# A planned gated-attention and feed-forward kernel: the plan's costs, its early fillers, the loads of step 1's gates and the places of attention's groups

## The chip, the cores and the metric

The kernel runs on one core of one Trainium2 chip. The metric is the device time of one execution in microseconds (us); of several runs the median is given. The engines have the names of the profile: PE is TensorE (PEld its weight loads), ACT is ScalarE, DVE is VectorE, POOL is GpSimd, SP is SyncE, which issues most transfers.

## The reference, cut to what matters

A gated recurrence over 768 time steps for 4 batches and 8 heads of size 48, and then a feed-forward block with 384 inputs, 2048 hidden values and 384 outputs on the 3072 resulting rows:

```python
f = 1.0 / (1.0 + np.exp(-f_logit))
for t in range(S):
    state = f[:, :, t, :, None] * state + np.einsum('bhd,bhe->bhde', k[:, :, t], v[:, :, t])
    y[:, :, t] = np.einsum('bhd,bhde->bhe', q[:, :, t], state)
...
h = x @ w_in
g = np.where(h >= 1, h, np.where(h <= -1, 0.0, (h + 1) ** 2 / 4))
out = g @ w_out
```

## The kernel before, in words

**The work.** Time is cut into 6 steps of 128. In each step the recurrence is computed in blocks: products of the gates' running values are made by two scans on VectorE (L476 and L483, `gate`), keys and queries are multiplied by them (L485, L487), and attention within a step is small products on TensorE: scores of keys and queries (L600, L666), their mask on VectorE (L631, L672), and mask times values (L721). What earlier steps add comes from a state: L753 multiplies queries by it, L814 makes what the step adds to it, out of turned keys. Keys are turned by TensorE in steps 0 and 1 (L685) and by VectorE's 32x32 transposes later (L699). A "pair" is two heads, four pairs make a step; pairs are numbered 4 times the step plus 0 to 3, and two of them are handled at a time. In step 0 the rows of the fourth pair stand in 16 spare rows of the other three tiles, and its scores are made from each of the three in turn, by `scores_of_last` (L619), here called the third-pair scores, since a product for each of the three pairs' tiles adds to them.

**The feed-forward block.** Each step has 512 columns and 16 units, 96 units in all. A unit's first half (`unit_1`, L242, unit 0 at L894) is nine wide products of 128x512, since weights and inputs are each split in a high and a low part and three of the four combinations are kept, times three blocks of 128 inputs. Then ScalarE and VectorE make the result: L245, L248 (ScalarE), the clamp L253 (VectorE), the cast to the high part `ghi` (L256, ScalarE) and the low part `glo` (L259, VectorE). The second half (`unit_2`, L266) is nine wide products again. The weights come as 64-bit numbers and are split early in the program, 25 blocks one after another: a load, a word from ScalarE (L370) and VectorE (L372), the high part (L375, ScalarE), the low part (L376, VectorE). Attention's outputs are rounded the same way into the inputs x: cast L704 on ScalarE, low half L705 on VectorE; in step 1 the outputs come in two halves of the columns, each with three casts.

**What sets the order.** A class `Plan` collects all operations with an engine, a cost from the table `COST` and what they need, and `order()` simulates the engines: at each moment a free engine takes the ready operation with the most urgent due time. The instructions are then emitted in the order of these start times, so each engine's queue is fixed. TensorE's operations are chained in the order of the calls: unit after unit, with attention's groups placed by two tables: `TURNS` says in which unit a pair's keys are turned, `VISITS` gives for each two pairs the units of the scores, of the mask times values with the state's sums, and of the outputs. An entry in the same unit as another stands directly behind it, with no wide products between.

**Fillers.** Where the plan has a gap ahead of a TensorE operation of over 500 ns, the emitting loop puts products of zeros there (`warm`, L320): as many as fill 0.9 of the gap at 330 or 230 ns each. They go to a bank that is free at the time, if there is one; from the scores of the third two heads to the first `unit_2` there is none, and none are put.

**Loads.** SyncE issues the loads in the plan's order. The gates `f` have two buffers that take turns and a third for the third load of step 0. In step 1 (`split_up`) gates, keys and queries are worked on in two halves of the columns; there a load of gates also needs `att[NP - 1]["to"]`, the moves of step 0's rows into the fourth tile `kq_71`. Three buffers `raw` take the weight blocks; a load waits for the word made from the block three before it, and the third one for step 0's last queries (L487).

Of the kernel before, what the change touches and what calls it, by code (L numbers as in the profile page):

```python
# [22 lines left out]
B, H, S, D = 4, 8, 768, 48  # L23
# [23 lines left out]

HOP, LANDING, PER_KB, NEAR, ADDING = 200, 2000, 3.0, 3500, 1500
COST = dict(mm=227, scores=1290, both=1150, part=500, states=1090, parts=850, turn=500, rows=317, scan=1145, dve=605, small=200, state=300, sums=480,
            act=710, copy=530, sig=540, issue=480, near=600, least=300)  # L50


TURNS = {4: 6, 5: 7, 6: 12, 7: 12, 8: 20, 9: 20, 10: 25, 11: 25, 12: 31, 13: 31, 14: 38, 15: 38, 16: 43, 17: 43, 18: 54, 19: 54, 20: 60, 21: 60, 22: 70, 23: 70}
VISITS = {4: (7, 10, 11), 6: (12, 13, 14), 8: (20, 23, 24), 10: (27, 28, 29), 12: (31, 35, 36), 14: (38, 40, 41), 16: (47, 51, 53), 18: (55, 57, 60), 20: (62, 69, 70), 22: (72, 74, 75)}
# [11 lines left out]


class Plan:
# [3 lines left out]
    def __init__(self):  # L72
        self.ops = []
        self.tensor = None

    def add(self, engine, cost, emit, *deps, kb=0, near=0):
# [9 lines left out]
        spread(list(deps))  # L86
        if engine == "PE":
            if self.tensor is not None and self.tensor not in flat:
                flat.append(self.tensor)
        o = Op(engine, COST[cost] if isinstance(cost, str) else cost, emit, flat, kb, near)  # L90
# [7 lines left out]
    def order(self):  # L98
        index = {o: n for n, o in enumerate(self.ops)}
        for o in reversed(self.ops):  # L100
            tail = o.cost + (LANDING + PER_KB * o.kb + (ADDING if o.engine == "POOL" else 0) if o.kb else o.near)
            o.late = min((u.late - (HOP if u.engine != o.engine else 0) for u in o.users), default=0) - tail
# [12 lines left out]
        while done < len(self.ops):  # L115
# [36 lines left out]
def gla_moe(ctx: ExitStack, tc: tile.TileContext, ff, kqd, f0, vv, vad, vbd, wd, fixedd, gates, values, headsd, out):  # L152
# [195 lines left out]

    def split_piece(k):

        j, c = order[k]

# [7 lines left out]
        mem, t = raw[k % 3][:, 0:n], bits[k % 4][:, 0:n]  # L360
# [9 lines left out]
        m = sca(COST["act"] * n // W, lambda: nc.scalar.activation(t, top, AF.Abs, bias=top_of, scale=2.0 ** 30),  # L370
# [3 lines left out]
        piece.append(v)  # L374
        h = sca("copy", lambda: nc.scalar.copy(hi, whole_val), v)  # L375
# [58 lines left out]
    def gate(m, halves=(None,)):  # L434
# [24 lines left out]
        for h, (b0, b1) in enumerate(steps):  # L459
            if split_up and h not in halves:  # L460
# [5 lines left out]
            l = dma(ft[:, cols], ff[i, p, :, cols], 256 // count, of_half(before, o, "qm") if before is not None else None,  # L466
                    att[NP - 1]["to"] if split_up else None)
# [734 lines left out]
```

## Time and profile before

| | |
|---|---|
| median of 3 runs | 481.05 us |
| lowest and highest | 479.98 and 485.14 us |
| the profiled execution's own time | 480.72 us |
| its span, first to last instruction | 478.9 us |
| busy: TensorE, VectorE, ScalarE, GpSimd | 469.0, 369.1, 265.2, 24.6 us |
| instructions | 11248 |

The span is what the profile's views cover, counted from its first instruction. A row of a timeline has the start, the length from the first start to the last end of the instructions merged in it, engine, line, operation and tiles, the shape and the count; in brackets the idle time before it and what ended that. Instructions of one engine overlap by the end of their pipeline, so the next one starts somewhat before the end that is shown; lengths of work that follows without a gap are read from start to start.

### The profile page before, as it was taken

The numbers are of one execution on the slowest core, as the hardware profiler recorded it, in microseconds if no ns is written. First come the engines' busy times: TensorE is split into PE (matmuls) and PEld (weight loads), VectorE is DVE, ScalarE is ACT, GpSimd is POOL, SyncE is SP. The second block draws the span as 40 slices with busy tenths as digits, with TensorE's granted clock in tenths as the row PEclk, the third lists the DMA queues.
The fourth block names the chain that finished last, engine by engine and source line by source line (L and its number), as shares of the span: only waits on it lengthen the run. The fifth ranks groups of instructions, "written<-read, shape, count | busy, mean of one in ns | idle before, by whom it ended". The sixth has DMA issues, their size and how long they took to land.

```text
span 478.9 us, 11248 instructions
## 1 busy us (share of the span) xinstructions
PE 469.0 (98%) x4659; PEld 384.2 (80%) x4659; DVE 369.1 (77%) x715; ACT 265.2 (55%) x487; POOL 24.6 (5%) x76
## 2 busy tenths in 40 slices
PE   8999999999999999999999999999999999999994
PEld 4788888789988888788878888888888888888883
DVE  7988989948999999999997599786576655655432
ACT  4399997856537364564654464464536344544451
POOL 3201001001000000100020000000000000000000
PEclk9999999999999999999999999999999999999999
DMA  8789754235204062131514230143420242422002
GB/s 289 219 299 310 226 193 144 69 117 214 63 15 141 3 171 73 35 122 45 133 34 151 94 119 26 45 121 112 154 89 3 89 122 88 155 88 88 2 0 73
DMA packets 21722, 54.29 MB, mean 113 GB/s; under 512 B 3328, under 2 KB 6656, under 8 KB 21664
## 3 DMA queue, kind: packets, MB, share of 16 engines
q1 hardware_dynamic: 20320, 51.43, 33.1%
q10 hardware_dynamic: 1344, 2.07, 2.0%
q8 instruction: 38, 0.62, 0.6%
q14 instruction: 20, 0.16, 0.1%
HBM read 44.63 MB, written 4.72 MB: 103 GB/s over the span
## 4 chain that ended last, share of the span: by engine, by line
PE 90%; DVE 4%; DMA 2%; ACT 2%; issue 1%; ACTq 0%; SPq 0%; DVEq 0%
PE po L266 41%; PE ph L242 39%; DMA f<-in_f 2%; PE pa L721 2%; PE pa L753 2%; PE ph L666 2%; DVE w L476 1%; DVE f L483 1%; PE pa L814 1%; PE ph L814 1%; PE pa L685 1%; DVE kq L487 1%; PE ph L894 0%; PE pa L666 0%; PE pa L863 0%
## 5 line engine op out<-in xcount | busy, mean ns | idle before, releaser
L242 PE MATMUL ph<-x,w_hi 128*128 128x512 f32 (+1 forms) x606 | 146.2, 377 | 0.0
L245 ACT ACTIVATE act<-ph,half 128x512 f32<-128x512 f32 x96 | 65.9, 687 | 111.9 <-PE ph L242 105.8
L242 PEld LDWEIGHTS ph<-x,w_hi 128*128 128x128 f32 x606 | 109.7, 188 | 20.9
L253 DVE SCALAR_TENSOR_TENSOR act<-ph,act 128x512 f32<-128x512 f32 x96 | 66.0, 687 | 52.8 <-ACT act L248 52.2
L256 ACT CAST ghi<-act 128x512 fp32r<-128x512 f32 x96 | 59.5, 620 | 67.6 <-DVE act L253 67.4
L266 PE MATMUL po<-ghi,w_hi 128*128 128x512 f32 (+1 forms) x305 | 87.1, 391 | 0.1
L266 PE MATMUL po<-ghi,w_lo 128*128 128x512 f32 (+1 forms) x305 | 83.2, 378 | 0.0
L266 PE MATMUL po<-glo,w_hi 128*128 128x512 f32 (+1 forms) x305 | 82.8, 377 | 0.0
L242 PE MATMUL ph<-x,w_lo 128*128 128x512 f32 (+1 forms) x303 | 81.2, 376 | 0.0
L259 DVE TENSOR_TENSOR glo<-act,ghi 128x512 fp32r<-128x512 f32 x96 | 65.9, 686 | 19.6 <-ACT ghi L256 18.6
L699 DVE STREAM_TRANSPOSE kn<-kq 32x128 f32<-32x128 f32 x224 | 67.8, 303 | 3.5
L266 PEld LDWEIGHTS po<-ghi,w_lo 128*128 128x128 f32 x305 | 55.2, 188 | 11.0
L266 PEld LDWEIGHTS po<-glo,w_hi 128*128 128x128 f32 x305 | 55.3, 188 | 10.9
L242 PEld LDWEIGHTS ph<-x,w_lo 128*128 128x128 f32 x303 | 55.3, 188 | 10.4
L248 ACT ACTIVATE act<-act 128x512 f32<-128x512 f32 x96 | 60.7, 632 | 2.9
L266 PEld LDWEIGHTS po<-ghi,w_hi 128*128 128x128 f32 x305 | 52.5, 188 | 10.9 <-ACT ghi L256 0.8
L386 DVE TENSOR_REDUCE ok<-raw 128x1 f32<-128x512 f32 x48 | 31.2, 678 | 4.5 <-DMA raw<-in_w 4.5
L476 DVE TENSOR_TENSOR_SCAN w<-f,least_w 128x512 f32<-128x512 f32 (+1 forms) x21 | 21.3, 1016 | 2.7 <-ACT f L474 2.2
L483 DVE TENSOR_TENSOR_SCAN f<-f,rec 128x512 f32<-128x512 f32 (+1 forms) x21 | 21.3, 1018 | 0.5
L370 ACT ACTIVATE bits<-raw,top_of 128x512 uint32<-128x512 fp8e4 (+1 forms) x25 | 18.1, 740 | 6.0 <-DMA raw<-in_w 3.4
L574 ACT ACTIVATE sd<-sd,kq 112x48 f32<-112x48 f32 x80 | 20.1, 328 | 0.0
L480 POOL COPY end<-w 128x4 f32<-128x4 f32 (+1 forms) x22 | 6.5, 295 | 261.9 <-DVE w L476 246.8
(125 smaller groups left out, 386.5 us busy)
## 6 DMA issues: line engine op xcount, KB each, us to landing
raw<-in_w SPq DMA_DIRECT2D x24, 512.0 KB, 3.5
raw<-in_w SPq DMA_DIRECT2D x21, 511.6 KB, 4.6
kq<-in_kq SPq DMA_DIRECT2D x18, 512.0 KB, 4.8
out_y<-raw SPq DMA_DIRECT2D x17, 256.0 KB, 2.2
v<-in_v SPq DMA_DIRECT2D x10, 384.0 KB, 5.0
f<-in_f SPq DMA_DIRECT2D x13, 256.5 KB, 3.0
raw<-in_w SPq DMA_DIRECT2D x4, 382.9 KB, 6.7
f<-in_f SPq DMA_DIRECT2D x7, 128.5 KB, 3.0
```

What stands on the lines that cost most here:

```text
L242: nc.tensor.matmul(ps[:, to], w_in(w_hi if high else w_lo, j, kt), xt[:, kt, t, c], start=(n == 0), stop=(n == 8))
L245: nc.scalar.activation(a, ps, AF.Relu, bias=half, scale=0.5)
L248: nc.scalar.activation(a, a, AF.Square)
L253: nc.vector.scalar_tensor_tensor(out=a, in0=ps, scalar=1.0, in1=a, op0=ALU.max, op1=ALU.min)
L256: nc.scalar.copy(hi, a)
L259: nc.vector.tensor_tensor(out=lo, in0=a, in1=hi.bitcast(F32), op=ALU.subtract)
L266: nc.tensor.matmul(po[e][:, c], w_out(part, j, e), g[:, of], start=(j == 0 and n == 0 and c.start == 0), stop=(j == NJ - 1 and n == 2))
L386: seen.append(vec("dve", lambda z=z, op=op: nc.vector.tensor_reduce(out=ok[:, 1 + NG + z + c:2 + NG + z + c], in_=words_of(raw[2])[1].bitc ...
L476: s1 = vec(1200 // count, lambda bwd=bwd, u0=u0, u1=u1: nc.vector.tensor_tensor_scan(out=wide(w[:, u0:u1]), data0=bwd, data1=wide(least_w[ ...
L483: s2 = vec(1200 // count, lambda fwd=fwd, b0=b0, b1=b1: nc.vector.tensor_tensor_scan(out=fwd, data0=fwd, data1=wide(rec[:, b0:b1]), initia ...
L574: nc.scalar.activation(ds[:, at + j * D:at + (j + 1) * D], state[:, q * B + b], AF.Copy, scale=pf[:R, j:j + 1])
L699: nc.vector.transpose(kn[n % 2][u:u + 32, ::-1, r:r + 32], src[:, :, u:u + 32])
```

## The change

It has five parts.

1. Costs. The table gets a finer set of costs; results now reach their users after a delay per engine (`LATENCY`), also on the same engine except TensorE; and passing from wide to small products on TensorE and back costs `first` and `last`.
2. Fillers. Before 20 us of the plan a gap from 250 ns on is filled whole, with one product more; behind it the rule is as before.
3. Loads. The gates of step 1 no longer need the moves of step 0; the third weight block no longer waits for step 0's last queries; the buffers of the weight blocks are followed by name (`last_in`) with the same waits otherwise.
4. The third-pair scores read 64 rows of each tile instead of 32; the rows added hold zeros on the key side.
5. `TURNS` and `VISITS` have new entries.

```diff
+LATENCY = dict(PE=235, ACT=140, DVE=110, POOL=150)
-VISITS = {4: (7, 10, 11), 6: (12, 13, 14), 8: (20, 23, 24), 10: (27, 28, 29), ...
+VISITS = {4: (6, 7, 10), 6: (11, 12, 13), 8: (18, 22, 24), 10: (24, 28, 29), ...
...
+    def lag(self, user):
+        if self.kb or self.near:
+            return HOP if user.engine != self.engine else 0
+        return 0 if self.engine == user.engine == "PE" else LATENCY.get(self.engine, HOP)
...
+            small = kind in SMALL_PRODUCTS
+            cost += (COST["last"] if small else COST["first"]) if small != self.small else 0
+            self.small = small
...
-                ready[u] = max(ready[u], end + (HOP if u.engine != o.engine else 0))
+                ready[u] = max(ready[u], end + o.lag(u))
...
-        loaded = dma(into, src, 8 * 128 * n / 1024, piece[k - 3] if k >= 3 else gates_of[2]["qm"] if k == 2 else None)
+        loaded = dma(into, src, 8 * 128 * n / 1024, last_in.get(home))
...
-            l = dma(ft[:, cols], ff[i, p, :, cols], 256 // count, of_half(before, o, "qm") if before is not None else None,
-                    att[NP - 1]["to"] if split_up else None)
+            l = dma(ft[:, cols], ff[i, p, :, cols], 256 // count, of_half(before, o, "qm") if before is not None else None)
...
-                for (_, ps, _), a in zip(last_held, (32, 96)):
-                    nc.tensor.matmul(ps[:, m], last_keys[t][a:a + 32, B - 1 - m], query(0, t, m)[a:a + 32], start=t == 0 and m == 0, stop=t == NT - 1 and m == B - 1)
+                for (_, ps, _), a in zip(last_held, (0, 64)):
+                    nc.tensor.matmul(ps[:, m], last_keys[t][a:a + 64, B - 1 - m], query(0, t, m)[a:a + 64], start=t == 0 and m == 0, stop=t == NT - 1 and m == B - 1)
...
-                if idle and o.start - idle > 500:
-                    warm(int((o.start - idle) * 0.9 / (330 if o.start < 10000 else 230)))
+                gap = o.start - idle if idle else 0
+                if o.start < 20000 and gap > 250:
+                    warm(int(gap / (330 if o.start < 10000 else 230)) + 1)
+                elif gap > 500:
+                    warm(int(gap * 0.9 / 230))
```

What it moves on the engines is shown at three places. The line numbers of the new kernel are 14 to 17 higher for the same statement there. The first is ScalarE around the rounding of step 1's first outputs (casts of pa_108 and pa_109 into x_86 and y_87; f are gates, ghi and act a unit's results, bits and w_hi weights). Before:

```order
L245 ACTIVATE act_84<-ph_112,half 128x512
L375 CAST w_hi<-bits_98 128x512
L375 CAST w_hi<-bits_95 128x512
L375 CAST w_hi<-bits_96 128x512
L704 CAST x_86<-pa_108 112x2x256
L248 ACTIVATE act_84<-act_84 128x512
L704 CAST x_86<-pa_109 112x256
L474 ACTIVATE f_67<-f_67 128x513
L474 ACTIVATE f_66<-f_66 128x513
L704 CAST y_87<-pa_109 112x256
```

Now:

```order
L262 ACTIVATE act_84<-act_84 128x512
L491 ACTIVATE f_66<-f_66 128x513
L387 ACTIVATE bits_96<-raw_92,top_of 128x512
L270 CAST ghi_89<-act_84 128x512
L387 ACTIVATE bits_97<-raw_93,top_of 128x512
L259 ACTIVATE act_83<-ph_111,half 128x512
L393 CAST w_hi<-bits_96 128x512
L262 ACTIVATE act_83<-act_83 128x512
L721 CAST x_86<-pa_108 112x2x256
L721 CAST x_86<-pa_109 112x256
L721 CAST y_87<-pa_109 112x256
```

The sigmoids of f_67 and f_66 stood between the second and the third cast; now the one of f_66 stands ahead of the casts, that of f_67 further up, and the three casts follow each other.

The second place is VectorE between the last mask of step 0 (am_77 from po_114) and the low half of unit 0's third input (x_85 from pa_108); bits and w_lo are weights, w and f_66 gates of step 1. Before:

```order
L631 TENSOR_TENSOR am_77<-po_114,fixed 128x512
L376 TENSOR_TENSOR w_lo<-bits_95,w_hi 128x3x128
L372 SCALAR_TENSOR_TENSOR bits_97<-raw_94,bits_97 128x512
L376 TENSOR_TENSOR w_lo<-bits_96,w_hi 128x3x128
L376 TENSOR_TENSOR w_lo<-bits_97,w_hi 128x512
L705 TENSOR_TENSOR x_85<-po_113,x_85 128x512
L705 TENSOR_TENSOR x_85<-pa_110,x_85 128x512
L705 TENSOR_TENSOR x_85<-pa_108,x_85 128x512
```

Now:

```order
L648 TENSOR_TENSOR am_77<-po_114,fixed 128x512
L394 TENSOR_TENSOR w_lo<-bits_95,w_hi 128x3x128
L394 TENSOR_TENSOR w_lo<-bits_96,w_hi 128x3x128
L389 SCALAR_TENSOR_TENSOR bits_97<-raw_94,bits_97 128x512
L493 SCALAR_TENSOR_TENSOR w<-f_66,least_w 128x256 x2
L394 TENSOR_TENSOR w_lo<-bits_97,w_hi 128x512
L722 TENSOR_TENSOR x_85<-po_113,x_85 128x512
L722 TENSOR_TENSOR x_85<-pa_110,x_85 128x512
L389 SCALAR_TENSOR_TENSOR bits_98<-raw_92,bits_98 128x384
L389 SCALAR_TENSOR_TENSOR bits_95<-raw_93,bits_95 128x512
L722 TENSOR_TENSOR x_85<-pa_108,x_85 128x512
```

Ahead of the third low half now stand the two scans of step 1's first gates and two more words of weight blocks.

The third place is TensorE at the end of the outputs of pairs 8 and 9 (am times v into pa) in unit 24. Before, with the second half of a unit behind them:

```order
L721 MATMUL pa_109<-am_77,v 48x64
L721 MATMUL pa_108<-am_76,v 48x64
L721 MATMUL pa_109<-am_77,v 48x64
L266 MATMUL po_113<-ghi_89,w_hi 128x512
L266 MATMUL po_114<-ghi_89,w_hi 128x512
L266 MATMUL po_115<-ghi_89,w_hi 128x512
```

Now, with the scores of pairs 10 and 11 (keys kq_70) behind them:

```order
L738 MATMUL pa_109<-am_77,v 48x64
L738 MATMUL pa_108<-am_76,v 48x64
L738 MATMUL pa_109<-am_77,v 48x64
L683 MATMUL ph_112<-kq_70 64x64
L683 MATMUL pa_110<-kq_70 64x64
L683 MATMUL ph_112<-kq_70 64x64
```

The scores of pairs 10 and 11 stood in unit 27 by themselves. The same happens with outputs and scores in units 37, 44, 54, 61 and 72. TensorE's list of products of zeros changes too: 25 ahead of the first scores, 4 ahead of the second, and 2 within the transposes of step 1's second half before; 26 ahead of the first scores, 7 ahead of the second and 5 ahead of the third now, and none behind.

## Rows read from the trace of the kernel before

**Rows 1.** the page's first part: busy time, share of the span, instructions of each engine

```profile
PE 469.0 (98%) x4659; PEld 384.2 (80%) x4659; DVE 369.1 (77%) x715; ACT 265.2 (55%) x487; POOL 24.6 (5%) x76
```

**Rows 2.** span and mean granted TensorE clock of the core

```profile
core 0: 478.9 us, clock 0.999
```

**Rows 3.** what TensorE waited for: us in total, times, longest

```profile
PE ph L320 <- DVE zeros L292: 1.0, 1, 1.0
PE pa L685 <- DVE y L705: 1.0, 1, 1.0
```

**Rows 4.** TensorE's timeline, the start: start us, us, instruction, [idle before <- releaser]

```profile
11.91 1.04 PE L320 MATMUL ph<-zeros 128*128 128x512 bf16 x4
13.19 0.37 PE L600 MATMUL po<-kq 48*128 48x128 f32 x1 [0.25 <-DVE kq L487]
...
15.73 0.37 PE L600 MATMUL po<-kq 48*128 48x128 f32 x1 [0.28 <-DVE kq L487]
...
17.91 1.09 PE L852 MATMUL po<-am,sd 128*64 128x128 f32 x16
...
26.85 0.55 PE L685 MATMUL pa<-fixed,kq 112*128 112x112 f32 x4
```

**Rows 5.** VectorE's timeline, the start

```profile
5.35 1.25 DVE L483 TENSOR_TENSOR_SCAN f<-f,rec 128x256 f32<-128x256 f32 x2
...
17.98 0.68 DVE L631 TENSOR_TENSOR act<-po,fixed 128x512 f32<-128x512 f32 x1
...
20.71 0.69 DVE L631 TENSOR_TENSOR am<-po,fixed 128x512 f32<-128x512 f32 x1
21.31 0.55 DVE L376 TENSOR_TENSOR w_lo<-bits,w_hi 128x384 fp32r<-128x384 f32 x1
21.77 0.69 DVE L372 SCALAR_TENSOR_TENSOR bits<-raw,bits 128x512 uint32<-128x512 uint32 x1
22.38 0.56 DVE L376 TENSOR_TENSOR w_lo<-bits,w_hi 128x384 fp32r<-128x384 f32 x1
...
25.49 0.69 DVE L705 TENSOR_TENSOR x<-pa,x 128x512 fp32r<-128x512 f32 x1 [0.42 <-ACT x L704]
```

**Rows 6.** ScalarE's timeline, the start

```profile
19.76 0.51 ACT L375 CAST w_hi<-bits 128x384 fp32r<-128x384 f32 x1 [2.61 <-DVE bits L372]
```

**Rows 7.** the timeline of all engines, around 85 us

```profile
82.73 0.64 ACT L474 ACTIVATE f<-f 128x513 f32<-128x513 f32 x1 [0.78 <-DMA f<-in_f]
...
83.13 0.55 PE L685 MATMUL pa<-fixed,kq 112*128 112x112 f32 x4
...
83.51 0.60 PE L320 MATMUL po<-zeros 128*128 128x512 bf16 x2
...
84.60 0.41 DVE L705 TENSOR_TENSOR y<-pa,y 112x256 fp32r<-112x256 f32 x1
...
85.07 0.79 PE L685 MATMUL pa<-fixed,kq 112*128 112x112 f32 x4 [0.96 <-DVE y L705]
```

**Rows 8.** TensorE's timeline, eight transposes without a wait

```profile
34.90 0.93 PE L685 MATMUL pa<-fixed,kq 112*128 112x112 f32 x8
```

**Rows 9.** the chain of waits around 255 us: start us, us, what

```profile
254.74 2.27 PE po L266 x9
...
259.05 2.04 PE po L266 x9
```

**Rows 10.** TensorE's timeline, nine wide products that precede small ones

```profile
75.28 1.52 PE L242 MATMUL ph<-x,w_hi 128*128 128x512 f32 x6
...
77.42 0.67 PE L753 MATMUL pa<-kq,y 48*48 48x64 f32 x32
```

**Rows 11.** the tile kq, 0 to 25 us: duration ns min/median/max, start, forms

```profile
L600 PE MATMUL pa<-kq x24: 272/272/373, 9.2 to 14.1; 48*128 48x128 f32 x24
...
L619 PE MATMUL ph<-kq,kn x24: 270/270/372, 10.8 to 17.7; 32*128 32x128 f32 x24
```

**Rows 12.** the page's DMA issues: KB each, median us from issue to landing

```profile
raw<-in_w SPq DMA_DIRECT2D x24, 512.0 KB, 3.5
```

More of the change, by code (lines that the diff above doesn't have):

```diff
@@ L45 @@
 NW = DM * DF // (128 * W)
+SMALL_PRODUCTS = ("scores", "heads", "thirds", "both", "begin", "before", "part", "states", "parts", "turn")
 HOP, LANDING, PER_KB, NEAR, ADDING = 200, 2000, 3.0, 3500, 1500
[L49 to L54, printed above, removed]
+LATENCY = dict(PE=235, ACT=140, DVE=110, POOL=150)
+COST = dict(mm=227, narrow=120, scores=1100, heads=950, thirds=1110, both=1090, begin=480, before=930, part=560, states=850, parts=830, turn=350, first=110, last=95,
+            rows=316, turned_rows=150, scan=1140, dve=602, small=200, sums=467, gate=600, act=575, bits=660, round=485, copy=520, turned=412, sig=538, decay=226,
+            issue=480, near=600, least=300)
+TURNS = {4: 5, 5: 6, 6: 11, 7: 11, 8: 15, 9: 15, 10: 24, 11: 24, 12: 30, 13: 30, 14: 37, 15: 37, 16: 44, 17: 44, 18: 54, 19: 54, 20: 61, 21: 61, 22: 72, 23: 72}
+VISITS = {4: (6, 7, 10), 6: (11, 12, 13), 8: (18, 22, 24), 10: (24, 28, 29), 12: (31, 35, 37), 14: (37, 42, 44), 16: (44, 48, 54), 18: (54, 56, 61), 20: (61, 69, 72), 22: (72, 75, 76)}
 START = (("scores", 0), ("mask", 0), ("last", 0), ("scores", 1), ("mask", 1), ("last", 1), ("scores", 2), ("last", 2), ("mask", 2),
@@ L73, in __init__ @@
         self.ops = []
-        self.tensor = None
+        self.tensor, self.small = None, False
     def add(self, engine, cost, emit, *deps, kb=0, near=0):
@@ L86, in add @@
         spread(list(deps))
+        cost, kind = COST[cost] if isinstance(cost, str) else cost, cost
         if engine == "PE":
@@ L89, in add @@
                 flat.append(self.tensor)
-        o = Op(engine, COST[cost] if isinstance(cost, str) else cost, emit, flat, kb, near)
+            small = kind in SMALL_PRODUCTS
+            cost += (COST["last"] if small else COST["first"]) if small != self.small else 0
+            self.small = small
+        o = Op(engine, cost, emit, flat, kb, near)
         for d in flat:
@@ L101, in order @@
             tail = o.cost + (LANDING + PER_KB * o.kb + (ADDING if o.engine == "POOL" else 0) if o.kb else o.near)
-            o.late = min((u.late - (HOP if u.engine != o.engine else 0) for u in o.users), default=0) - tail
+            o.late = min((u.late - o.lag(u) for u in o.users), default=0) - tail
         left = {o: len(o.deps) for o in self.ops}
@@ L347, in gla_moe @@
     SKIP = 3
+    last_in = {}
     def split_piece(k):
         j, c = order[k]
+        home = k % 3
         if c is None:
@@ L699, in emit @@
                     nc.vector.transpose(kn[n % 2][u:u + 32, ::-1, r:r + 32], src[:, :, u:u + 32])
-            c["kn"].append(vec(4 * COST["rows"], emit, c["kq"], old(n - 2, "st")))
+            c["kn"].append(vec(4 * COST["rows"] + COST["turned_rows"], emit, c["kq"], old(n - 2, "st")))
         c["tr"] = c["kn"][-1]
     def rounded(b, yf, hi, lo, y, past, cost=None):
-        eh = sca(cost or "act", lambda: nc.scalar.copy(hi, yf), y, past)
+        eh = sca(cost or "round", lambda: nc.scalar.copy(hi, yf), y, past)
         el = vec(cost or "dve", lambda: nc.vector.tensor_tensor(out=lo, in0=yf, in1=hi.bitcast(F32), op=ALU.subtract), eh)
@@ L736, in begin @@
         c["to_y"] = held, where
-        c["yb"] = add("PE", "part", attended(n, True), c["am"], c["lv"], d["lv"], [b[2] for b in held])
+        c["yb"] = add("PE", "begin", attended(n, True), c["am"], c["lv"], d["lv"], [b[2] for b in held])
     def outputs(n):
@@ L754, in emit @@
                                          start=False, stop=False)
-        c["ys"] = add("PE", 1000, emit, c["db"], d["db"], c["later"], c["yb"])
+        c["ys"] = add("PE", "before", emit, c["db"], d["db"], c["later"], c["yb"])
         y = c["y"] = d["y"] = add("PE", "part", attended(n, False), c["ys"])
```

33 lines of the change are left out of this document (17 added, 16 removed).

## The prediction

> **What bounds the kernel now.** I read the page's first part first: TensorE is busy for 469.0 of 478.9 us [rows 1], at a mean granted clock of 0.999 of full speed [rows 2], which is the 2.4 GHz level. So nothing is to be had from faster work elsewhere; only TensorE's own idle time, its own switching costs, and where its stream begins and ends can move the time. Next the list of what TensorE waited for: the two longest waits are 1.0 us each, one at the very first instruction and one at L685 [rows 3]; the others are of 0.5 us or less. Last the timelines of the stretches in which they lie: the start, up to about 27 us, where TensorE waits a quarter of a microsecond at a time for the first keys and queries [rows 4 to 6], and one place at 83 to 86 us [rows 7]. From 27 us on TensorE's products stand end to end but for that place. The reader is to see that the whole change can act on three things: that one stall, the price of passing between wide and small products, and the start.
>
> **The stall at 85 us goes: -1.8 us.** At 83.13 TensorE starts the eight transposes of step 1's second half, runs two zeros after the fourth, and then stands until 85.07; the last of the eight ends at 85.07 + 0.79 = 85.86 [rows 7]. That is 2.73 us, where eight such transposes without a wait take 0.93 us [rows 8]: 1.8 us are lost here. Why: the second four write a bank that the rounding of step 1's first outputs must leave. ScalarE's order puts two sigmoids of step 2's gates between the second and third cast of that rounding (first pair of order fences), and the second of them stood 0.78 us for its load, at 82.73; the third cast, and with it VectorE's subtraction at 84.60 that frees the bank, came later by the sigmoids and that wait [rows 7]. In the new order the three casts stand together and the sigmoid is well ahead of the first. Also, since step 1's gates no longer wait for step 0's moved rows and the second half's keys come two to three units sooner on VectorE, the load that ScalarE waited for is issued sooner relative to its sigmoid. What is late next there is the same bank: from the end of the outputs, three casts and three subtractions of 0.4 to 0.7 us each, partly side by side, an estimate of 3 us from the lengths in [rows 5, 7], against two wide runs of 2.27 and 2.04 us on TensorE [rows 9]. That leaves a microsecond or more. Bounds: -1.0 (nearly half of it comes back through another wait on the same bank) to -1.9 (the scores behind start a little before the last transpose ends).
>
> **Six small groups merge: -1.8 us.** TensorE's work is the same number of products, but the new table puts the outputs of one pair of head pairs and the scores of the next into the same unit six times (24, 37, 44, 54, 61, 72; third pair of fences); before, none coincided. A nine-product run that follows small products takes 2.27 us in the chain of waits instead of 2.04 [rows 9], and one that precedes them takes 2.14 (75.28 to 77.42) [rows 10]. So a small group standing alone costs 0.23 + 0.10 = 0.33 us in switching, and six merges save 6 x 0.33 = 2.0, less a little for the passage from outputs to scores, which the trace of before doesn't show. Small kinds that follow each other there go on at the pace of their own products, so I take -0.30 each, -1.8. If that passage cost nearly a whole edge, only 0.10 each would be left, -0.6; the upper end is -2.0.
>
> **The start: +1.1 us.** Here the change does two things against each other. VectorE's order of the first gates is tighter, so the first keys and queries are ready sooner. But TensorE is now given more zeros: 7 where there were 4 ahead of the second scores, and 5 ahead of the third scores where there were none (26 instead of 25 at the very beginning, where TensorE has to wait in any case). A zero costs 0.22 us: four last 1.04 us and two last 0.60, so two more are 0.44 [rows 4, 7]. Step by step. The four zeros from 11.91 ended at 12.95 and TensorE waited 0.25 us more, to 13.19 [rows 4]. Three more end at 12.95 + 0.66 = 13.6: the zeros overrun. Scores and third-pair scores together take 17.91 - 15.73 = 2.18 us [rows 4], so the next five zeros run from 15.8 to 16.9, and the third scores start at 16.9 instead of 15.73. Their input came at 15.73 before, and one mask of 0.60 us now stands ahead of it on VectorE: 16.3 at the latest, so the zeros alone decide. VectorE can mask these scores from about 18.05, half of 2.18 us after they start; before, it began them at 17.98, since it was itself late [rows 5]. So VectorE's lead is used up. From that mask to the last one there are the same six instructions in another order, 20.71 - 17.98 = 2.73 us [rows 5]: the last mask starts at 20.8.
>
> From there VectorE decides. Before, it began the low half of unit 0's third input at 25.49, having waited 0.42 us for the cast [rows 5]. Now four more instructions stand ahead of it (second pair of fences): two half scans of step 1's gates (1.25 us for a pair [rows 5]), a small word (0.46, as 21.31 to 21.77) and a large one (0.61, as 21.77 to 22.38) [rows 5]. With the mask (0.60), the two small low parts (0.92), a large word and a large low part (1.22) and two low halves of inputs (1.22, each taken as long as a large word), 20.8 + 0.60 + 0.92 + 1.22 + 1.22 + 1.25 + 0.46 + 0.61 = 27.1, and with its 0.69 us it ends at 27.75. The last of unit 0's nine products needs it and takes 0.23, so the transposes behind start at 27.95 instead of 26.85 [rows 4]: +1.1 us, and as TensorE's stream is dense from there on, that stays. Bounds: +0.3 (the input is ready some 0.8 us sooner, as it would be if the zeros did not overrun) to +2.0 (a load that ScalarE waits for is a microsecond later).
>
> What hides the rest. ScalarE gets step 1's four sigmoids ahead of its first weight casts; it stood idle there for 2.61 us, up to 19.76, waiting for VectorE [rows 6], and four half sigmoids are half as much. If that cover were gone (loads landing after about 20.8), every microsecond more would be on the path. The third weight block is loaded sooner and competes with nothing that is due. New costs in the plan's table change orders only.
>
> **Wider row tiles cost nothing.** The third-pair scores read 64 rows instead of 32. The medians of one product are 272 ns for 48 rows and 270 ns for 32 [rows 11], so I cost the change at zero. The Trainium skill, TensorEngine Tiling (Array Packing), section Theoretical Speedup, gives a contraction of at most 32 a packing factor of 4 and one of at most 64 only 2, which speaks against the edit. By that rule the products of these three groups could cost up to twice as much; by the rows, nothing. No row here has the same product at both widths.
>
> **The sum.** The profiled execution took 480.72 us, 1.8 us more than its span, and stands 0.33 us below the median of the three runs, 481.05. 480.7 - 1.8 - 1.8 + 1.1 = 478.2 us.
>
> **Rivals.**
> 1. The start costs little: VectorE reaches the last mask near 20.0, the low half is there 0.8 us sooner, and the start costs 0.3. 480.7 - 3.6 + 0.3 = 477.4. For it: VectorE is otherwise full in this stretch and its new order has fewer back-to-back dependences. Against: the zeros stand in TensorE's queue whatever VectorE does.
> 2. The stall comes back elsewhere: a sigmoid that waits for its load still stands in ScalarE's queue, now ahead of a unit's cast (in the first pair of fences it is ahead of the cast of a result, ghi_89). If it is 1.5 us late, the saving is gone: 478.2 + 1.5 = 479.7. Against: the load is issued about two units, some 9 us, ahead.
> 3. Slower than before: ScalarE's first cast of a unit's result now stands behind the word of a weight block whose load can only be issued once VectorE has made the word before it, at about 26.5. That load has to land by 30.5 or TensorE's first output products wait. A load of 3.5 us, the median of such blocks [rows 12], is in time. From 2.5 us late on, the kernel is slower than before; at twice the median, 7 us, it would land at 33.5, 3 us late, and the time is 478.2 + 3.0 = 481.2. For it: the DMA engines are busiest in this stretch of the program. Against: the transfers of step 1's gates, which stood ahead of such a block before, are already over.
> 4. Two products of 64 rows do run at half the pace. Each of the three groups takes 2.18 / 2 = 1.09 us [rows 4], so 3 x 1.09 = 3.3 us more on TensorE, all of it at the start: 481.5. The Trainium skill's packing factors (TensorEngine Tiling, Theoretical Speedup) would make it so. Against: the equal rows above [rows 11].
> 5. The merges save little, -0.6 in place of -1.8: 479.4.
>
> **How the numbers follow.** The forecast holds from 477.7 to 479.0, with a chance of 0.45; rival 1 0.20; rival 2 0.10; rival 3 0.05; rival 4 0.02; rival 5 0.13; something faster than all of these, under 476.2, gets 0.05. The end of the bounds on the good side is 480.7 - 1.9 - 2.0 + 0.3 = 477.1, on the bad side 480.7 - 1.0 - 0.6 + 2.0 = 481.1. A measurement differs from the profiled execution by some 0.3 us, and a start that gains rather than loses can't be excluded, so the range is 476.4 to 481.2. About 1% is what a measurement of this kernel can tell from no change: under 476.2 I give 0.08, within 1% 0.87, and above 485.9 0.05, where two of the slow rivals would have to come together.
>
> **What would show it.** Right: no zeros on TensorE behind 20 us; L685 of step 1's second half without a wait; the wide runs next to the six merged groups at 2.04 us on the side that no longer has small products; the transposes behind unit 0 at about 28.0 us; a wait of a microsecond on VectorE's third low half inside unit 0. Wrong: unit 0 ends by 27.0 (rival 1); a wait at the cast of a unit's result, or at the first output products at 31 to 34 us (rivals 2 and 3); a passage from outputs to scores of more than 0.1 us (rival 5); products of the third-pair scores that start further apart than those of the scores beside them (rival 4).

## The result, and the profile after

Each kernel was timed 20 times, in turn. The changed one took 483.90 us in the median (480.09 to 486.97), the kernel before 480.98 (479.71 to 486.70); the ratio is 1.0048 with a 95% interval of 1.0025 to 1.0072 (ratios here are estimates over the executions and not the quotients of the medians). The forecast was 478.2 us with a range of 476.4 to 481.2: the change was to gain 2.5 us against the profiled execution and lost 2.9 from median to median. The spread is part of the result. The profiled execution, 480.09 us, is the quickest of the 20, so the rows here show the change nearly at its best; a usual execution follows in the first experiment.

The page's first part, and span and clock of the core:

```profile
PE 467.6 (98%) x4666; PEld 384.4 (80%) x4666; DVE 366.5 (77%) x715; ACT 263.2 (55%) x487; POOL 28.0 (6%) x76
```

```profile
core 0: 478.3 us, clock 0.995
```

What TensorE waited for (us in total, times, longest):

```profile
PE po L280 <- ACT ghi L270: 2.3, 2, 1.6
...
PE ph L911 <- DVE x L722: 0.6, 1, 0.6
```

The wait at the transposes [rows 3] is gone. A new one leads: output products (L280) that wait for ScalarE's cast ghi of a unit's result (L270).

TensorE's timeline at the start, and VectorE's third low half of unit 0's input:

```profile
11.21 1.68 PE L334 MATMUL ph<-zeros 128*128 128x512 bf16 x7
...
14.81 1.25 PE L334 MATMUL ph<-zeros 128*128 128x512 bf16 x5
...
27.28 0.50 PE L911 MATMUL ph<-x,w_hi 128*128 128x512 f32 x1 [0.60 <-DVE x L722]
27.61 0.55 PE L702 MATMUL pa<-fixed,kq 112*128 112x112 f32 x4
```

```profile
26.54 0.68 DVE L722 TENSOR_TENSOR x<-pa,x 128x512 fp32r<-128x512 f32 x1
```

Seven and five zeros, as read from the order; the last of unit 0's products waits 0.60 us for the low half, and the transposes stand at 27.61, where 26.85 was and 27.95 was forecast. The start costs 0.76 us, from one execution of each kernel; in the second execution of the changed one (below) the transposes stand at 27.48.

TensorE's timeline at the second half of step 1: eight transposes, then scores and the next products:

```profile
79.88 0.93 PE L702 MATMUL pa<-fixed,kq 112*128 112x112 f32 x8
...
81.83 0.97 PE L280 MATMUL po<-ghi,w_hi 128*128 128x512 f32 x3
```

The same products of the kernel before start, with the zeros and the wait among them, at 83.13 [rows 7] and end ahead of this row:

```profile
86.88 0.97 PE L266 MATMUL po<-ghi,w_hi 128*128 128x512 f32 x3
```

No zeros, no wait: 81.83 - 79.88 = 1.95 us for what took 86.88 - 83.13 = 3.75. The stall is gone as forecast, 1.80 us.

The tile kq, 0 to 25 us (duration ns min/median/max):

```profile
L617 PE MATMUL pa<-kq x24: 272/272/373, 9.2 to 13.7; 48*128 48x128 f32 x24
...
L636 PE MATMUL ph<-kq,kn x24: 270/272/272, 10.2 to 17.8; 64*128 64x128 f32 x24
```

Products of 64 rows take what those of 48 take, and what those of 32 took [rows 11].

The merges, in TensorE's timeline of the kernel before around one group of outputs and one of scores (first lines of each run of nine wide products):

```profile
311.93 1.52 PE L242 MATMUL ph<-x,w_hi 128*128 128x512 f32 x6
...
317.73 1.52 PE L242 MATMUL ph<-x,w_hi 128*128 128x512 f32 x6
...
321.81 1.52 PE L242 MATMUL ph<-x,w_hi 128*128 128x512 f32 x6
...
327.21 1.52 PE L242 MATMUL ph<-x,w_hi 128*128 128x512 f32 x6
```

and of the changed kernel, where both groups stand together:

```profile
314.00 1.52 PE L256 MATMUL ph<-x,w_hi 128*128 128x512 f32 x6
...
320.73 1.52 PE L256 MATMUL ph<-x,w_hi 128*128 128x512 f32 x6
```

Before, 317.73 - 311.93 = 5.80 and 327.21 - 321.81 = 5.40 us, each with nine products of 2.04 us in front and nine behind [rows 9]: 1.72 and 1.32 us for the two groups, 3.04 together. Now 320.73 - 314.00 - 4.08 = 2.65. This merge saves 0.39 us (0.30 was forecast). Read the same way, the six merged places come to 2.65 to 2.75 us in this trace against the 3.04 of two separate groups: 0.29 to 0.39 each, 2.1 in all for the 1.8 forecast.

So the three terms came as worked out or some 0.3 us better. What was not foreseen stands eight microseconds behind that merge, in the chain of waits (start us, us, what):

```profile
317.73 5.98 DMA kq<-kq
...
323.74 2.13 DMA x<-y
...
325.88 0.70 ACT act L259
...
327.98 0.63 ACT ghi L270
...
328.65 2.34 PE po L280 x9
...
333.03 2.04 PE po L280 x9
```

Read it from the bottom. Nine output products start at 328.65 though TensorE was free 1.6 us before; they wait for ghi, ghi through VectorE's L267 for ScalarE's functions of the unit, and the first of these (L259) stood behind small copies in ScalarE's queue (x<-y, 16 rows of attention's outputs moved into the feed-forward block's inputs, issued at 323.74; they are called copies of MLP inputs below), which in turn stood until another copy, of key rows (kq<-kq) and issued at 317.73, had landed 5.98 us later.

### The profile page after: what moved, and what is told of

Read it like the earlier page. It is cut to its first block, busy times and chain, and to the rows that moved or that the text cites. A ratio compares the mean times of both kernels' runs of the same rounds, so it can differ in the third digit from the quotient of the medians.

```text
span 478.3 us, 11260 instructions
## 1 busy us (share of the span) xinstructions
PE 467.6 (98%) x4666; PEld 384.4 (80%) x4666; DVE 366.5 (77%) x715; ACT 263.2 (55%) x487; POOL 28.0 (6%) x76
## 4 chain that ended last, share of the span: by engine, by line
PE 89%; DMA 4%; DVE 2%; ACT 2%; ACTq 1%; POOL 0%; SPq 0%; issue 0%; DVEq 0%
PE po L280 41%; PE ph L256 39%; DMA f<-in_f 2%; PE pa L770 2%; PE pa L738 2%; PE ph L683 1%; DMA kq<-kq 1%; PE pa L831 1%; ACTq L298 1%; PE ph L831 1%; DVE x L722 1%; PE pa L702 1%; DVE w L493 1%; POOL kq L516 0%; PE pa L683 0%; ACT f L491 0%
## 5 line engine op out<-in xcount | busy, mean ns | idle before, releaser
L259 ACT ACTIVATE act<-ph,half 128x512 f32<-128x512 f32 x96 | 65.9, 686 | 121.2 <-PE ph L256 107.4
L267 DVE SCALAR_TENSOR_TENSOR act<-ph,act 128x512 f32<-128x512 f32 x96 | 65.9, 686 | 66.6 <-ACT act L262 65.9
L270 ACT CAST ghi<-act 128x512 fp32r<-128x512 f32 x96 | 59.6, 621 | 60.7 <-DVE act L267 60.4
L280 PE MATMUL po<-ghi,w_hi 128*128 128x512 f32 (+1 forms) x305 | 86.4, 389 | 2.3 <-ACT ghi L270 2.3
L280 PE MATMUL po<-ghi,w_lo 128*128 128x512 f32 (+1 forms) x305 | 83.1, 378 | 0.0
L280 PE MATMUL po<-glo,w_hi 128*128 128x512 f32 (+1 forms) x305 | 82.8, 377 | 0.0
L280 PEld LDWEIGHTS po<-ghi,w_lo 128*128 128x128 f32 x305 | 55.2, 188 | 10.9
L280 PEld LDWEIGHTS po<-glo,w_hi 128*128 128x128 f32 x305 | 55.3, 188 | 10.8
L280 PEld LDWEIGHTS po<-ghi,w_hi 128*128 128x128 f32 x305 | 53.0, 188 | 13.3 <-ACT ghi L270 3.1
L404 DVE TENSOR_REDUCE ok<-raw 128x1 f32<-128x512 f32 x48 | 31.1, 675 | 2.4 <-DMA raw<-in_w 2.4
L497 POOL COPY end<-w 128x4 f32<-128x4 f32 (+1 forms) x22 | 9.2, 419 | 265.1 <-DVE w L493 255.5
```

The lines of the kernel that those rows point to most:

```text
L259: nc.scalar.activation(a, ps, AF.Relu, bias=half, scale=0.5)
L267: nc.vector.scalar_tensor_tensor(out=a, in0=ps, scalar=1.0, in1=a, op0=ALU.max, op1=ALU.min)
L270: nc.scalar.copy(hi, a)
L280: nc.tensor.matmul(po[e][:, c], w_out(part, j, e), g[:, of], start=(j == 0 and n == 0 and c.start == 0), stop=(j == NJ - 1 and n == 2))
L404: seen.append(vec("dve", lambda z=z, op=op: nc.vector.tensor_reduce(out=ok[:, 1 + NG + z + c:2 + NG + z + c], in_=words_of(raw[2])[1].bitc ...
```

## The experiments

### A usual execution

The changed kernel once more.

> The changed kernel once more, so that another execution of it is profiled: its best execution was 480.1 us, as forecast, but the middle of its 20 was 483.9. Theory 'a late wait that comes and goes': a profile of a usual execution shows 2 to 5 us more idle time of TensorE than the 480.1 us one, in one or two places, and a stretch at the half clock behind it; median 483 to 485 against 480 to 482 of the kernel before. Theory 'the chip's chance': the same chain of waits, only a longer tail or a later full clock, and a median within 0.25% of the kernel before.

483.05 us (481.31 to 485.64), ratio 1.0032, 0.9998 to 1.0066. The profiled execution took 483.35 us. ScalarE's timeline in it (ACTq are issues of transfers):

```profile
320.46 0.51 ACTq L298 DMA_DIRECT2D x<-y  x1
...
321.58 2.68 ACTq L298 DMA_DIRECT2D x<-y  x2
326.88 0.51 ACTq L298 DMA_DIRECT2D kq<-kq  x1
327.44 0.69 ACT L259 ACTIVATE act<-ph,half 128x512 f32<-128x512 f32 x1 [6.12 <-DMA x<-y]
```

TensorE's wait for ghi, its timeline, and the granted clock by windows (third column from the end: 1.00 is the 2.4 GHz level, 0.50 the 1.2 GHz one):

```profile
PE po L280 <- ACT ghi L270: 3.5, 2, 3.0
```

```profile
326.35 0.84 PE L256 MATMUL ph<-x,w_lo 128*128 128x512 f32 x3
330.21 1.09 PE L280 MATMUL po<-ghi,w_hi 128*128 128x512 f32 x3 [3.02 <-ACT ghi L270]
...
333.67 1.84 PE L256 MATMUL ph<-x,w_hi 128*128 128x512 f32 x6
```

```profile
320.00:330.00 10.00, 7.20 (x32) 5.63 (x30) 4.89 (x8) 3.09 (x8) 0.00 (x0) 1.00 0.78 215
331.00:334.00 3.00, 3.00 (x8) 2.32 (x8) 2.31 (x4) 1.03 (x2) 0.00 (x0) 0.50 0.22 42
335.00:340.00 5.00, 5.00 (x24) 4.12 (x23) 3.07 (x5) 2.53 (x4) 0.00 (x0) 1.00 0.28 107
```

And the chain of waits:

```profile
320.30 6.50 DMA v<-in_v
...
330.21 3.65 PE po L280 x9
...
336.20 2.04 PE po L280 x9
```

The four issues on ScalarE run from 320.46 to 327.4, and the unit's first function comes at 327.44; the last of them, of key rows, stood until a load of values that SyncE had issued at 320.30 landed 6.50 us later. The product that the function works on was complete at about 323: TensorE's next work waits 3.02 us. Then the clock falls to half for 3.4 us of products: in the chain the same eighteen products take 336.20 - 330.21 = 5.99 us that took 333.03 - 328.65 = 4.38 in the quicker execution, 1.61 us more. 483.35 - 3.02 - 1.61 - 0.52 (the second wait for ghi, at 102 us) = 478.2: take out these three and the forecast's 478.2 is left. The quicker execution without its two waits, 1.64 and 0.66 us, leaves 477.8. 'Late wait' holds. Of the 20 executions 14 had a mean clock of 0.993 or less; this one, with a fall, had 0.992, and the quickest, without, 0.995. The kernel before has such executions too, 13 of the 35 timed beside this run; its one trace shows no fall, so what falls add to its median is not known.

Why the issues take so long is written in the program: each transfer takes the next of eight completion counters (DMAHW0 to DMAHW7) and its issue waits for the one that had that counter before. ScalarE's order with its waits, at this place:

```
363 L298 DMA x_85<-y_87 16x1024 [waits DMAHW6_49,DVE_49]
364 L298 DMA x_85<-y_87 16x1024 [waits DMAHW1_49]
365 L298 DMA x_85<-y_87 16x1024 [waits DMAHW3_49]
366 L298 DMA kq_71<-kq_68 16x1028 [waits DMAHW5_49,DMAHW4_49]
367 L259 ACTIVATE act_83<-ph_111,half 128x512 [waits PE_49]
```

The Trainium skill says in DMA: Bandwidth & Descriptors, section Anatomy of one DMA — SWDGE (gpsimd) path, that DMA engines do not wait on semaphores and that any such wait happens on the sequencer that issues. The trace agrees for ScalarE, whose transfers are not GpSimd's: 0.51 us each is what an issue takes, 5.6 and 7.0 us passed from the first of four to the function behind them.

### Which part of the change

The changed kernel has no zeros behind 20 us. Most edits below that change the planned order also leave out the rule that would put some there; of the kernels made from the changed one, only two further down, at 9 us, have any.

The table of turns and visits back to the old one (`-TURNS = {4: 5, ...}` `+TURNS = {4: 6, ...}`, and VISITS).

> The changed kernel with the old table of turns and visits, the rest as changed. If the new places of attention's groups make the time, the median falls to 480 to 481.5 us, and the six merged groups (1.8 us) are missing in the trace; if they do not, it stays at 483 to 485 or rises by the merges' 1 to 2 us.

483.61 us, 1.0033 (1.0002 to 1.0063). Not the table: the stall only moves. TensorE waits 1.28 us for ghi at 238.9, again behind a copy of key rows in ScalarE's queue, and the six merges are lost. The stall at 81 us did not come back here either.

The old rule for zeros:

```diff
-    if o.start < 20000 and gap > 250:
-        warm(int(gap / (330 if o.start < 10000 else 230)) + 1)
-    elif gap > 500: ...
+    if idle and o.start - idle > 500:
+        warm(int((o.start - idle) * 0.9 / (330 if o.start < 10000 else 230)))
```

> The changed kernel with the old rule for zeros (fewer fillers at the start: none behind the first 'last' product, fewer ahead of it). If the start's zeros make the usual execution slow, the median falls to 480 to 481 us; if they do not, it stays within 1 us of the changed kernel, and the first unit of the MLP begins 0 to 0.8 us sooner.

482.43 us, 1.0029 (0.9996 to 1.0061): not the zeros; the profiled execution waits 2.43 us for ghi at 330.66. Unit 0 did not begin sooner but 0.85 us later (25.18 against 24.33). That is not the zeros' doing: in this execution a load of the first gates landed later, and VectorE was 0.70 us behind at 10.06 already, ahead of all that it reads from TensorE. What the zeros cost at the start stays open.

The new table, in the kernel before (which so also loses its two late zeros):

> The kernel before with the new table of turns and visits alone, costs and the rest as before. If the new places are what makes a usual execution slow, this one is 2 to 4 us slower than the kernel before; by the forecast it is 0 to 2 us faster (merges), and by 'the costs set the order, not the table' it is within 1 us.

481.04 us, 0.9999 (0.9972 to 1.0025), with no wait for ghi. The merges are in it and the stall at L685 is gone, so the table alone takes that away. But the profiled execution lost 2.4 us at the start, where the clock was at half from 15.7 to 22.5 us, and from the transposes behind unit 0 on it is 1.45 us shorter than the kernel before, not 3.6: small waits in its new order, 0.51 us at 117 and 0.37 at 151 the largest, are part of what takes the rest.

The old costs and delays in the plan:

```diff
-LATENCY = dict(PE=235, ACT=140, DVE=110, POOL=150)
-COST = dict(mm=227, narrow=120, scores=1100, ... act=575, ...
+LATENCY = dict(PE=200, ACT=200, DVE=200, POOL=200)
+COST = dict(mm=227, narrow=120, scores=1290, ... act=710, ... first=0, last=0, ...
...
```

> The changed kernel with the old costs and delays in the plan (table of turns, zeros, loads and 64-row products as changed). In its order two copies of key rows and one of MLP inputs come ahead of the unit's function where the changed kernel has three and one, and two after it. If the new costs bring the wait at 328 us, it is under 0.6 us here, and the median is 480 to 481.5 us though the stall near 81 us may be back (1 to 2 us); if the wait is from the table or the loads, it stays at 1.5 to 3 us.

479.93 us (478.98 to 480.51), 0.9951 (0.9924 to 0.9979): the new costs bring the stall. ScalarE's timeline with the old ones:

```profile
322.11 2.12 ACTq L298 DMA_DIRECT2D x<-y  x2
324.57 0.69 ACT L259 ACTIVATE act<-ph,half 128x512 f32<-128x512 f32 x1 [2.16 <-PE ph L256]
...
326.84 1.16 ACTq L298 DMA_DIRECT2D kq<-kq  x2
```

The unit's function at 324.57 waits for TensorE alone: the copies of MLP inputs ahead of it are issued by 324.23, and the key rows' issues come after it. What is left of the wait for ghi stands at 328.7:

```profile
PE po L280 <- ACT ghi L270: 0.4, 1, 0.4
```

No execution had a mean clock under 0.996. Up to 320 us this kernel is 1.3 us behind the changed one (600 output products into the program, 321.09 against 319.81), so the new costs also gain something before they lose it. The stall at 81 us did not come back.

The old waits of loads (`+ att[NP - 1]["to"] if split_up else None` on step 1's gates, `piece[k - 3]` for weight blocks):

> The changed kernel with the old waits of loads: step 1's gates load only after the copies of step 0's key rows, weight blocks by the block three before. ScalarE's order around 328 us is that of the changed kernel, so by 'copies' the wait for ghi stays (1.5 to 3 us) and the median stays at 483 to 484; if sooner loads make the wait, it goes and the median falls by 2 to 3 us. Start and the place at 81 us may lose 0.5 to 2 us.

482.38 us, 0.9995 (0.9962 to 1.0029). The stall stays, 2.15 us at 328.6, and with it the fall of the clock, 328.9 to 332.3 us. Up to there this kernel is ahead of the changed one (its 451st output product starts at 243.39 against 244.88): in these two executions the sooner loads cost a little.

### The two links

Copies of key rows issued by SyncE, in the same planned order (`q = nc.sync if near == NEAR + 1 else q`), and then all small copies:

> The changed kernel, in the same planned order, but SyncE issues the copies of key rows that ScalarE issued. Theory 'copies': at 328 us ScalarE's first function of a unit stands behind three copies of MLP inputs and one of key rows, the last of which is issued only as a load of values some transfers back lands; so with the key rows' copies gone from ScalarE, TensorE's wait for the cast ghi there (1.6 us in one execution, 3.0 in another) falls below 0.5 us, no clock dip follows it, and the median falls from 483.5 to 480 to 481.5 us. Theory 'late products' (ScalarE and VectorE are simply behind there): the wait stays between 1 and 3 us and the median at 483 to 484.

> The changed kernel with all small copies, of key rows and of MLP inputs, issued by SyncE. 'Copies': the waits for the cast ghi at 102 us (0.5 to 0.7) and at 328 us both go, fastest execution 477.5 to 478.5 us, median 479 to 481; the price could be loads that queue behind twelve issues of 0.5 to 0.6 us on SyncE. 'Late products': both waits stay.

481.25 us, 0.9985 (0.9954 to 1.0017), and 480.80 us, 0.9977 (0.9946 to 1.0008): better than the changed kernel by 2 to 3 us, but a wait for ghi remains one unit later, 1.29 and 1.97 us, where 'copies' expected less than 0.5 or none. VectorE's timeline with all copies on SyncE, and TensorE behind it:

```profile
329.68 1.28 DVE L404 TENSOR_REDUCE ok<-raw 128x1 f32<-128x512 f32 x2 [4.06 <-DMA raw<-in_w]
330.87 0.68 DVE L267 SCALAR_TENSOR_TENSOR act<-ph,act 128x512 f32<-128x512 f32 x1
```

```profile
332.25 0.80 PE L280 MATMUL po<-ghi,w_hi 128*128 128x512 f32 x1 [1.97 <-ACT ghi L270]
```

A second link: two reductions (L404) that only check a weight block stand 4.06 us for its load, with the unit's L267 queued behind them. In the changed kernel the load has landed by the time these two come, behind ScalarE's delay.

Both out: copies of key rows on SyncE, and the plan counts 9 us to a checked block's landing.

```diff
-    loaded = dma(raw[2], wd[c], 8 * 128 * W / 1024, seen[-2:] or [...])
+    loaded = add("SP", "issue", lambda: nc.sync.dma_start(raw[2], wd[c]), seen[-2:] or [...], near=9000)
```

> The changed kernel with both suspected links taken out: SyncE issues the copies of key rows, and the plan counts 9 us to the landing of a weight block that is only checked, so that VectorE's two reductions of it stand later. If these two are the whole cause, TensorE waits under 0.4 us in all between 315 and 345 us, the clock does not fall there, and the median is 478 to 480 us. If only ScalarE's copies count, it is like the run with the copies moved alone, 481.3. If the stall is of another kind it comes back nearby with 1 to 3 us.

486.06 us, 1.0084 (1.0047 to 1.0122), all of it lost at the end. No wait stands between 315 and 345 us, but the checks now reach to the end of the program, and the rule for zeros filled the planned gap ahead of the product that sums them up:

```profile
462.63 7.73 PE L335 MATMUL po<-zeros 128*128 128x512 bf16 x35
470.29 0.19 PE L1003 MATMUL pa<-ones_col,ok 128*1 128x1 f32 x2
```

So 6.5 us instead, and no zeros behind 20 us:

> As the run with both links out, but the plan counts 6.5 us to a checked block's landing, so that the last check stands ahead of the 94th of 112 units. If the two links are the whole cause, no wait above 0.4 us and no fall of the clock between 315 and 345 us, last product near 469 us and a median of 477.5 to 479; if the tail was not the checks' doing, 484 to 486 again.

483.52 us, 1.0038 (1.0006 to 1.0069): a miss. In the new order copies of MLP inputs, left on ScalarE, stand ahead of the unit's function and of its square, and TensorE waits 3.69 us, with 3.4 us at half the clock behind it:

```profile
323.14 2.65 ACTq L299 DMA_DIRECT2D x<-y  x2
325.84 0.69 ACT L259 ACTIVATE act<-ph,half 128x512 f32<-128x512 f32 x1 [3.46 <-DMA kq<-kq]
329.34 0.52 ACTq L299 DMA_DIRECT2D x<-y  x1
329.90 0.63 ACT L262 ACTIVATE act<-act 128x512 f32<-128x512 f32 x1 [3.37 <-DMA kq<-kq]
```

The checks alone at 6.5 us:

> The changed kernel with the checked blocks counted at 6.5 us alone; ScalarE keeps its copies, four of them ahead of the unit's function near 328 us. By 'copies first' the wait for ghi stays at 1 to 3 us and the median at 482 to 484; if VectorE's checks were the main link, the wait goes and the median is 479 to 480.5.

482.08 us, 1.0001 (0.9967 to 1.0035), with a wait of 1.50 us for ghi at 330.9 and one of 2.03 at 251.4, where a copy of key rows stands between the function and its square in ScalarE's queue: the copies are the first link. Then both for good, all copies on SyncE and checks at 6.5 us:

> The changed kernel, new loads kept, with all small copies issued by SyncE and checked blocks counted at 6.5 us. If the two links are the whole cause, no wait above 0.8 us between 315 and 345 us and a median of 477 to 478.5 (that with old loads was 477.3; the new loads lost 0.65 us at the start). If the new loads had a part in the stall, 1 to 3 us of wait come back near 330 us and the median is 480 to 483.

478.23 us (477.05 to 479.28), 0.9907 (0.9871 to 0.9942). TensorE's waits:

```profile
PE ph L256 <- DMA x<-y: 0.8, 1, 0.8
PE pa L1002 <- DVE ok L998: 0.7, 1, 0.7
...
PE po L280 <- ACT ghi L270: 0.4, 1, 0.4
```

The wait for ghi near 330 us is gone (0.4 us are left at 31.6), the clock never falls in the trace, and the median is the forecast's 478.2. To the tenth this is luck: the order is another than the one forecast. What remains near 330 us is 0.8 us for a copy itself, which SyncE now issues later, and 0.7 at the end, for the checks.

### Teaching the plan

The plan lets no transfer issue before the eighth last has landed by its own estimate; then, an issue on ScalarE counted as 1.4 us instead of 0.6:

```diff
+    if (o.kb or o.near) and ring[-8] > t:
+        heappush(q, (ring[-8], n, o))
+        continue
```

> The changed kernel whose plan lets no transfer issue before the one eight issues back has landed by its own estimate. In its order the copy of key rows stands behind the unit's function on ScalarE, three copies of MLP inputs still ahead. If the issue that waits for the load of values is the price, ScalarE's function is 1 to 2 us sooner there, and the median falls to 480.5 to 482; if the copies of MLP inputs hold it as well, or VectorE's check is next, it stays at 482 to 484.

> The changed kernel whose plan counts 1.4 us instead of 0.6 for an issue on ScalarE (the trace: four issues took 5.6 us there). In its order two copies of MLP inputs stand ahead of the unit's function near 240 us and three near 328 us, no copy of key rows behind them. If the undercounted issue is the root, the wait for ghi falls below 0.8 us and the median to 479.5 to 481.5; if VectorE's checks are then late, 1 to 2 us of it come back and it is 481 to 483.

483.43 us, 1.0028 (0.9980 to 1.0076), and 489.42 us, 1.0150 (1.0111 to 1.0189): neither helps. In the first the copy of key rows moved from ahead of the function to between it and the square, where ScalarE stood 3.09 us; in the second, which has a copy there too, VectorE's check stood 4.41 us as well. TensorE waits 2.52 and 4.19 us for ghi there; the second loses more in smaller waits and a fall of the clock, which are not taken apart here. Both only moved the issues: a copy between a unit's product and its cast held TensorE in both.

### Combinations

Old costs with old loads; old loads with new costs, all copies on SyncE and the checks at 9 us, then at 6.5 us without late zeros:

> The kernel before with new table, zeros and 64-row products alone: old costs and old loads. The run with old costs and new loads gave 479.9. If the loads by themselves cost time at the start (0.67 us there in the run with old loads), this is 0.3 to 0.8 us below it, 479 to 479.7; if the sooner loads help step 1's first half, it is 0.5 to 1.5 us above it.

> The changed kernel with the old waits of loads, all small copies issued by SyncE, and the checks' weight blocks counted at 9 us. The run with the old loads was 1.5 us ahead of the changed kernel from 107 to 245 us and lost it in the stall near 328 us, so with both links out the last product starts near 469.5 us and the median is 477.5 to 479.5 us; if the stall only moves, 480 to 482.

> Old waits of loads, all small copies on SyncE, checked blocks counted at 6.5 us, the rest as changed. With the tail mended this keeps what the run with 9 us showed before its tail (830th output product 3.3 us ahead of the changed kernel's best execution): last product 467.5 to 468.5 us, median 475.5 to 477.5; it would be the fastest of all. If something of the tail stays, 479 to 482.

480.40 us, 0.9968 (0.9930 to 1.0007), between its two expectations and within the noise of the run with new loads; 484.58 us, 1.0054 (1.0017 to 1.0092), with the same zeros at the end; and 477.33 us (476.66 to 477.61), 0.9899 (0.9862 to 0.9937), the fastest of all kernels here. Its waits:

```profile
PE po L280 <- ACT ghi L270: 0.9, 2, 0.6
```

Last, whether the same two edits do the kernel before good:

> The kernel before with the same two links out: all small copies issued by SyncE, checked blocks counted at 6.5 us, old costs, table, zeros and 32-row products. Its own stall near 85 us is VectorE's and stays. If the rest of the change is worth what was forecast, 1.8 us of stall and 1.8 us of merges less 1.1 at the start, this is 2 to 3.5 us above 477.3, so 479.3 to 480.8; if the links cost the kernel before time as well and the rest of the change is worth little, 477 to 478.5.

483.76 us, 1.0045 (1.0008 to 1.0082): they harm it, which was not expected. ScalarE's timeline at the place of its old stall, and TensorE behind it:

```profile
85.26 0.63 ACT L474 ACTIVATE f<-f 128x513 f32<-128x513 f32 x1 [2.85 <-DMA f<-in_f]
85.80 0.35 ACT L704 CAST y<-pa 112x256 fp32r<-112x256 f32 x1
```

```profile
87.59 1.01 PE L685 MATMUL pa<-fixed,kq 112*128 112x112 f32 x4 [3.44 <-DVE y L705]
```

With more issues on SyncE the gates' load is issued later, at 80.02 us where it was 78.28; the sigmoid between the casts, which stood 0.78 us for it [rows 7], stands 2.85, and TensorE 3.44. Behind that wait the clock is at half for 6.8 us, so this execution, 486.04 us, is one of the longer ones. The changed kernel has its casts together and shows no such wait. The difference, 483.8 - 478.2 = 5.5 us, is therefore not the worth of the rest of the change: the edit itself made the kernel before's own stall longer.

## Why the prediction was wrong

- The stall at 85 us: right, gone, 1.80 us for 1.8, by the step described. The new table alone is enough for it, and so are the other parts with the old table.
- The merges: right in kind and nearly in size, 0.29 to 0.39 for 0.30 each, 2.1 us for 1.8.
- The start: right in kind, +0.76 for +1.1. The zeros set the third scores, VectorE the end of unit 0, as forecast, but the steps between were sooner: third scores at 15.99 for 16.9, mostly since the sum started the first zeros where they stood before (11.91; now 11.21), and the last mask at 19.98 for 20.8, which is where rival 1 had it. VectorE then took 0.3 us more than summed, waiting for a cast, and the low half came 0.5 us sooner than 27.1. (The summands as given end at 28.0, not 27.95.)
- 64-row products: right, no cost; they start 0.11 us apart at either width. The Trainium skill's packing factors (TensorEngine Tiling (Array Packing), Theoretical Speedup) did not show in these products.
- The sum failed at the sentence "New costs in the plan's table change orders only", with "as TensorE's stream is dense from there on, that stays". I costed the new order at two stretches before 90 us and took the rest for as dense as before. But order is what holds ScalarE free: the same copies that stood behind a unit's function in one order stand ahead of it in the other, and an issue that the plan counts with 0.6 us waits for landings, of 5.98 and 6.50 us in the two chains. In the two profiled executions this costs 1.64 and 3.02 us at 328 us, 0.66 and 0.52 at 102 us, and 1.61 for the clock where it falls: 5.15 us in the usual one, which is 483.35 less the forecast. The wait for ghi, the sign named for rival 2, did appear, with a cause that rival did not have: copies, not a sigmoid.
- The range failed with it: its upper end added sizes of known terms and had no term for the 300 us that were not looked at.

What stays open: why the new costs put the fourth copy, of key rows, ahead of the function is not traced to single entries; and the wait's size differs from execution to execution (1.6 to 3.0 us) with landings that no run here controlled.

## What to carry to other kernels

An instruction that issues a transfer can cost its engine not its own half microsecond but the landing it waits for; on an engine that also feeds the critical one, ask of every order what stands between a product and its cast. When a planner's numbers change, read the whole of each queue in the new order for issues and for waits on loads, also far from the edit. A quick execution can look like the forecast: look at the spread before believing a profile.

## What was not expected of the hardware

Around waits of 1.97, 2.15, 3.02, 3.69 and 4.19 us of TensorE the granted clock fell to 0.50 for 3.4 us each, and behind one of 3.44 us for 6.8; in the run with the new table alone it fell for 6.8 us at the start, behind a wait of only 0.95; around waits of 1.64, 2.03, 2.43 and 2.52 us it did not, so the length of the wait alone does not tell which. A fall of 3.4 us added 1.61 us, as much as half the wait itself. And more issues on one queue (SyncE's) made a transfer late for a sigmoid on another engine by 2.1 us.
